# One core, attention, routed MLP and bilinear block: raw weight blocks side by side, split weights stored once and later, two units' weights made during attention, y stores issued by ScalarE

## The chip, the cores and the metric

The kernel runs on one core of one Trainium2 chip. The metric is the device time of one execution in microseconds (us). Of the kernel before, three timed runs gave a median of 2388.02 us (2387.21 to 2389.52).

## The reference

Three stages follow one another. The first is an attention with a decaying state, over 4 batches, 8 heads, 768 steps and head size 48:

```python
f = 1.0 / (1.0 + np.exp(-f_logit))
for t in range(S):
    state = f[:, :, t, :, None] * state + np.einsum('bhd,bhe->bhde', k[:, :, t], v[:, :, t])
    y[:, :, t] = np.einsum('bhd,bhde->bhe', q[:, :, t], state)
```

Its output, 3072 tokens by 384, goes through a layer of 8 experts that all compute on all tokens. The weights of the sum come from `P`, eight rounds of normalising rows and columns (Sinkhorn) of `exp(x @ w_gate)`:

```python
for e in range(E):
    h = np.maximum(x @ w1[e], 0.0)          # 384 -> 1024
    out += P[:, e:e + 1] * (h @ w2[e])      # 1024 -> 384
```

The last stage is `((x @ w_a) * (x @ w_b)) @ w_out` with a width of 1536. Its three weights arrive as 64-bit floats and are turned into 32-bit ones on the chip.

## The kernel before, in words

**Arithmetic.** Every matrix product of weights and activations is made of three TensorE passes over operands split into a high and a low part (`h` and `l` in the tile names): high by high, high by low, low by high. ScalarE makes a high part (a copy), GpSimd or VectorE the low part (a difference).

**Two plans.** The program is written as a list of steps (`Plan.add`: priority, engine, estimated cost, what is read and written, the call, and `late`, the time after which a transfer counts as landed). `Plan.order` (L116) walks through them with the estimated costs and fixes the order in which each engine gets its instructions; each engine then runs its list strictly in order and waits on semaphores. There are two plans. The first (L364 to L856) holds attention in 24 steps of 128 tokens, the MLP of expert 0 for each pair of steps (`expert0`, L648, all of its blocks but the last) and the start of the normalising of `P` (`sinkhorn`, L696). The second (L863 to L1101) holds everything else. All transfers of the kernel before are issued by the SP queue; its estimated cost of an issue lies between 0.05 and 1.09 us, and `LATE` is 4.0 us.

**Units of the second plan.** Its work is cut into 81 jobs (L747). A job of kind `moe` takes three blocks of 128 hidden columns for 1024 tokens; there are 19 of them for each of three groups of tokens. A job of kind `out` does the same for `w_a` or `w_b`. The order is: 19 moe jobs, 19 moe jobs, 8 out jobs, 19 moe jobs, 16 out jobs. A job's *front* (`front`, L902) computes three hidden blocks by two halves of 512 tokens with 15 products (`CHAINS`, L43) instead of 18, from 15 sums of activation blocks (tiles `xsh`, `xsl`) and 15 sums of weight blocks (tiles `w1h`, `w1l`; two sets, used in turn). ScalarE copies a product out of its bank pG (`z<-pG`), or VectorE adds it to another. The *back* (`back`, L979) splits the hidden blocks (`gh`, `gl`), multiplies by the second weight (`w2h`, `w2l`, from a 192 KB load into `raw`) in banks pR, and VectorE adds the result to `acc`. The back of a job is planned beside the front of a later one.

**Weights of a job.** Only the first time a weight unit is used are its sums made. Nine raw blocks of 128x128 go to nine of the 15 slots of the tile `stage`, in three steps (`W_RAW`, L23; `w1_load`, L762). For `moe` a step loads three blocks, each in two transfers of 64 rows (`moe_rows`, L271), so that a unit has 18 transfers of 32 KB. GpSimd makes 13 sums of slots (`W_SUMS`, `w1_split`, L786). Then, in three groups of five slots (`W_GROUPS`), ScalarE makes `w1h`, GpSimd makes `w1l`, and SP stores each half to HBM (`wfmoe..h`, `wfmoe..l`): six stores of 320 KB for a unit, planned right behind the group's split. Later jobs with the same unit load these stored parts, in six loads.

**Around the border of the two plans.** In attention the first unit's weights are made and 9 of the 15 activation sums (`NXA`, L201). The other six and unit 1's weights follow at the head of the second plan. Four of the eight normalising rounds are in the first plan (`ROUNDS1`). Expert 0's result is stored to HBM as `y0` by SP (L683), and loaded into `acc` by the second plan. The tiles of the second plan lie where those of attention lay, and wait for their last readers.

Of the kernel before, what the change touches and what calls it, by code (L numbers as in the profile page):

```python
# [22 lines left out]
W_RAW = [[14, 13, 8], [5, 1, 9], [6, 12, 3]]  # L23
W_SUMS = [
    (0, 1, "subtract", 9),
    (2, 3, "subtract", 0),
    (0, 0, "add", 8),
    (4, 9, "add", 3),
    (4, 4, "add", 5),
    (7, 5, "subtract", 8),  # L30
    (10, 14, "add", 6),
    (11, 10, "add", 13),
    (10, 10, "add", 8),
    (9, 2, "subtract", 11),
    (9, 9, "subtract", 12),
    (14, 14, "add", 13),
    (14, 5, "subtract", 14),
]
W_GROUPS = [(0, 5), (5, 10), (10, 15)]
# [44 lines left out]
class Plan:  # L84
# [11 lines left out]
    def __init__(self):  # L96
        self.ops = []
        self.last = {}
# [17 lines left out]
    def order(self, share):  # L116
# [15 lines left out]
        while any(todo.values()):  # L132
# [24 lines left out]
            for u in users[n]:  # L157
                gap = late + (self.GAP if self.ops[u][1] != eng else 0.0 if eng == "PE" else self.SAME)
# [8 lines left out]
def kernel(  # L167
# [33 lines left out]
    NXA = 9  # L201
# [6 lines left out]
    ROUNDS1 = 4  # L208
# [19 lines left out]
    w1s = [[big.tile([128, NW, 128], F32R, name=f"w1{x}0") for x in "hl"]]  # L228
# [47 lines left out]
    def add_piece(plan, prio, key, parts, hj, lj, reads=()):  # L276
# [10 lines left out]
        plan.add(prio, "SP", .05 + m * .0013, reads, [rk], get, LATE)  # L287
# [110 lines left out]
    def attention(s):  # L398
# [230 lines left out]
        op(ACT, .37, [f"xf{z}"], [xk], lambda: nc.scalar.activation(out=hi, in_=xf, func=AF.Copy))  # L629
# [18 lines left out]
    def expert0(b):  # L648
# [22 lines left out]
        for tt in range(EB // 128):  # L671
# [11 lines left out]
            op(SP, .55, [ky], [], lambda ys=ys, tt=tt: nc.sync.dma_start(  # L683
# [78 lines left out]
    def w1_load(plan, prio, n):  # L762
# [4 lines left out]
        if first_of[kind, u] != n:  # L767
            for g, (lo, hi) in enumerate(W_GROUPS):
                for x, t in enumerate((wh, wl)):
                    plan.add(prio + W_STEP * g, SP, .1, [f"wf{kind}{u}{x}{g}"], [f"w1{n % 2}{g}"], partial(  # L770
                        nc.sync.dma_start, out=f32(t[:, lo:hi]), in_=wfd[kind][u][x][:, lo:hi]), LATE)
            return
        for kk, slots in enumerate(W_RAW):
            def get(kk=kk, slots=slots):
                for slot, (e, c) in zip(slots, blocks):
                    if kind == "moe":
                        parts = moe_rows(e, c, 128)[kk]
                    else:
                        parts = [(0, 128, wd[e][kk * 128:kk * 128 + 128, c:c + 128])]
                    for p0, k, src in parts:  # L780
                        nc.sync.dma_start(out=stage[p0:p0 + k, slot, :], in_=src)  # L781

            reads = [f"wd{ab}"] if kind == "out" else []
            plan.add(prio, SP, .38, reads, [f"sg{x}" for x in slots], get, LATE)

    def w1_split(plan, prio, n):  # L786
# [10 lines left out]
        for g, (lo, hi) in enumerate(W_GROUPS):  # L797
# [7 lines left out]
            for x, t in enumerate((wh, wl)):  # L805
# [336 lines left out]
```

## Time and profile before

| what | value |
|---|---|
| median of 3 runs | 2388.02 us |
| the profiled execution | 2391.95 us |
| its span, first to last instruction | 2390.2 us |
| TensorE busy | 2204.8 us, 92% |
| VectorE, ScalarE, GpSimd busy | 70%, 44%, 47% |
| mean granted TensorE clock | 0.962 |

In the page, PE is TensorE, DVE VectorE, ACT ScalarE, POOL GpSimd, SP the SyncE queue (SPq its issuing of transfers); L1101 is the line from which the second plan's steps are called, so that most of that plan's instructions carry it and are told apart by their tiles. TensorE's share is an average over stages. The table by stage, with busy times, clock and transfers, shows where it is lower, and the waits say what ended its idle time there. Idle time of another engine costs nothing by itself.

### The profile page before, as it was taken

To read this page: it belongs to the slowest core of one execution; us is meant where nothing else is said; L and a number is where in the kernel's file an instruction comes from. 1 tells how busy PE (TensorE), PEld (TensorE's weight loads), DVE (VectorE), ACT (ScalarE), POOL (GpSimd) and SP (SyncE) were. 2 spreads that over 40 slices of the span, in tenths; PEclk is the share of its full clock that TensorE was granted. 3 is DMA by queue.
4 is the path that set the end of the run, shared out by engine and by line. 5 is a ranking of instruction groups with operands and counts; after the bars stand their busy time and mean duration, and the time that the engine had idled before them with its cause. 6 is when DMAs were issued, how large, how long until landed. Compare 5 with 4: busy or idle time off the path is not lost.

```text
span 2390.2 us, 41604 instructions
## 1 busy us (share of the span) xinstructions
PE 2204.8 (92%) x15100; PEld 1968.6 (82%) x15100; DVE 1673.1 (70%) x2939; ACT 1050.0 (44%) x2059; POOL 1114.3 (47%) x1127
## 2 busy tenths in 40 slices
PE   4999889978899889999889999999999999999998
PEld 3888788857777778898779998888899999988887
DVE  6888889655676766768998877668655555656755
ACT  3544555543333433453334446445444444533432
POOL 4112341156774655536553337774533333645522
PEclk5899999988999999999999999999999999999999
DMA  6445654244554434556665444547643333556641
GB/s 147 101 89 128 152 125 89 56 131 147 175 184 134 138 130 132 175 183 217 226 190 177 147 148 151 183 150 249 229 132 112 115 116 100 171 180 206 219 139 41
DMA packets 360206, 359.18 MB, mean 150 GB/s; under 512 B 154560, under 2 KB 261312, under 8 KB 360000
## 3 DMA queue, kind: packets, MB, share of 16 engines
q1 hardware_dynamic: 360000, 356.52, 49.0%
q8 instruction: 119, 1.95, 0.4%
q14 instruction: 87, 0.71, 0.1%
HBM read 252.19 MB, written 99.48 MB: 147 GB/s over the span
## 4 chain that ended last, share of the span: by engine, by line
PE 50%; DVE 7%; DMA 2%; POOL 2%; SPq 2%; issue 1%; ACT 0%; POOLq 0%; DVEq 0%; ACTq 0%
PE pR L310 26%; PE pG L924 18%; PE pF L924 6%; DVE z L1101 3%; SPq L781 1%; DVE gl L1101 1%; POOL stage L1101 1%; DMA z<-in_moe_w_b_dram 1%; POOL w1l L1101 1%; DVE z L257 1%; DVE acc L1101 0%; DVE z L259 0%; DMA stage<-in_moe_w_dram 0%; DVE xsl L1101 0%; DVE z L261 0%
## 5 line engine op out<-in xcount | busy, mean ns | idle before, releaser
L310 PE MATMUL pR<-w2h,gl 128*128 128x384 f32 x1656 | 567.3, 343 | 2.5 <-POOL gl L1101 2.0
L310 PE MATMUL pR<-w2l,gh 128*128 128x384 f32 x1656 | 566.5, 342 | 0.0
L310 PE MATMUL pR<-w2h,gh 128*128 128x384 f32 x1656 | 562.6, 340 | 3.4 <-ACT gh L1101 3.2
L1101 ACT ACTIVATE z<-pG 128x512 f32<-128x512 f32 x474 | 281.2, 594 | 460.9 <-PE pG L924 438.9
L924 PE MATMUL pG<-xsh,w1h 128*128 128x512 f32 x891 | 363.0, 407 | 100.7 <-ACT z L1101 60.0
L1101 POOL TENSOR_TENSOR gl<-z,gh 128x512 fp32r<-128x512 f32 x219 | 296.2, 1365 | 322.6 <-ACT gh L1101 232.2
L1101 DVE SCALAR_TENSOR_TENSOR acc<-pR,prob,acc 128x384 f32<-128x384 f32 x528 | 320.4, 611 | 147.2 <-PE pR L310 142.6
L924 PE MATMUL pG<-xsl,w1h 128*128 128x512 f32 x891 | 357.8, 402 | 0.9 <-DVE xsl L1101 0.9
L924 PE MATMUL pG<-xsh,w1l 128*128 128x512 f32 x891 | 356.6, 400 | 1.7 <-POOL w1l L1101 1.7
L310 PEld LDWEIGHTS pR<-w2h,gh 128*128 128x128 f32 x1656 | 316.3, 191 | 46.9 <-ACT gh L1101 3.8
L310 PEld LDWEIGHTS pR<-w2l,gh 128*128 128x128 f32 x1656 | 315.8, 191 | 40.2
L268 POOL TENSOR_TENSOR w2l<-raw,w2h 128x384 fp32r<-128x384 f32 x207 | 226.5, 1103 | 247.0 <-ACT w2h L266 237.6
L310 PEld LDWEIGHTS pR<-w2h,gl 128*128 128x128 f32 x1656 | 316.4, 191 | 4.1 <-POOL gl L1101 3.1
L1101 ACT ACTIVATE gh<-z 128x512 fp32r<-128x512 f32 x414 | 248.4, 624 | 144.5 <-DVE z L1101 85.2
L1101 DVE TENSOR_TENSOR z<-pF,z 128x512 f32<-128x512 f32 x324 | 222.1, 687 | 92.1 <-PE pF L924 61.7
L924 PEld LDWEIGHTS pG<-xsh,w1h 128*128 128x128 f32 x891 | 170.3, 191 | 134.2 <-ACT z L1101 70.9
L1101 DVE TENSOR_TENSOR z<-z,pG 128x512 f32<-128x512 f32 x243 | 166.2, 684 | 113.8 <-PE pG L924 110.0
L1101 POOL TENSOR_TENSOR stage<-stage 128x128 f32<-128x128 f32 x338 | 162.7, 511 | 168.8 <-DMA stage<-in_moe_w_dram 147.4
L1101 DVE SCALAR_TENSOR_TENSOR gl<-z,gh 128x512 fp32r<-128x512 f32 x171 | 165.3, 977 | 66.2 <-ACT gh L1101 66.2
L924 PEld LDWEIGHTS pG<-xsh,w1l 128*128 128x128 f32 x891 | 170.1, 191 | 41.0 <-POOL w1l L1101 2.2
L1101 DVE TENSOR_TENSOR z<-pG,z 128x512 f32<-128x512 f32 x174 | 119.8, 688 | 116.1 <-PE pG L924 113.2
L667 POOL TENSOR_TENSOR hl<-hf,hh 128x256 fp32r<-128x256 f32 x84 | 74.4, 887 | 248.8 <-ACT hf L665 215.8
(168 smaller groups left out, 3657.1 us busy)
## 6 DMA issues: line engine op xcount, KB each, us to landing
raw<-in_moe_w_dram SPq DMA_DIRECT2D x178, 192.0 KB, 2.8
l<-x2d SPq DMA_DIRECT2D x45, 256.0 KB, 3.4
stage<-in_moe_w_dram SPq DMA_DIRECT2D x342, 32.0 KB, 2.1
l<-x1d SPq DMA_DIRECT2D x32, 256.0 KB, 3.2
raw<-wd SPq DMA_DIRECT2D x36, 192.0 KB, 3.0
nat_f<-in_f_logit_dram SPq DMA_DIRECT2D x24, 192.0 KB, 3.5
nat_q<-in_q_dram SPq DMA_DIRECT2D x24, 192.0 KB, 3.7
nat_k<-in_k_dram SPq DMA_DIRECT2D x24, 192.0 KB, 4.0
```

What stands on the lines that cost most here:

```text
L257: lambda: stt(out=f32(t), in0=lo.bitcast(U32), scalar=2.0 ** -52, in1=f32(t), op0=ALU.mult, op1=ALU.mult),
L268: plan.add(prio + 1, "POOL", .1 + m * .0026, [gk, key], [key], lambda: nc.gpsimd.tensor_tensor(out=lj, in0=got, in1=f32(hj), op=ALU.subtract))
L310: nc.tensor.matmul(out=ps, lhsT=a[:, off:off + 128], rhs=b, start=(start and i == 0), stop=(stop and i == n - 1))
L667: op(POOL, .64, [f"hh{ft}", kf], [f"hl{ft}"], lambda hh=hh, hl=hl, hf=hf: nc.gpsimd.tensor_tensor(out=hl, in0=hf, in1=f32(hh), op=ALU.subt ...
L781: nc.sync.dma_start(out=stage[p0:p0 + k, slot, :], in_=src)
L924: nc.tensor.matmul(out=ps, lhsT=a[:, x], rhs=b, start=(new and i == 0), stop=(i == 2), skip_group_check=not new)
L1101: fn()
```

## The change

- A unit's raw blocks lie side by side in `stage`: slots 12 to 14, 3 to 5 and 6 to 8. Blocks of one expert that follow one another make one run, and a run is loaded in one transfer (two for `moe`, of 64 rows by 384 columns, 96 KB). A unit inside one expert has 6 transfers instead of 18; four of the units 2 to 18 (5, 8, 13 and 16) cross a border of experts and have 12. `W_SUMS` is renamed to the new slots, `W_OF` says in which slot a product's weight lies, and the groups have 6, 4 and 5 slots.
- The split weights are stored in two transfers of 983 KB (all 15 slots), planned at two thirds of the job that uses them, after its product 9, instead of six right after the split. The next split into the same set of tiles waits for these stores.
- The first two units' weights are made in attention, after steps 14 and 17, and not stored there. In exchange 5 instead of 9 activation sums are taken in attention and 10 at the head of the second plan, through tiles `z`, seven of them with VectorE.
- Two normalising rounds are in attention and six in the second plan.
- Expert 0's result is stored by ScalarE's queue.
- The plan's estimated costs of SP issues are changed, and its gap between engines in the second plan is 0.4 instead of 0.2.

```diff
-W_RAW = [[14, 13, 8], [5, 1, 9], [6, 12, 3]]
+W_OF = [0, 4, 1, 8, 2, 3, 6, 9, 14, 5, 10, 11, 7, 13, 12]
+W_RAW = [12, 3, 6]
...
-W_GROUPS = [(0, 5), (5, 10), (10, 15)]
+W_GROUPS = [(0, 6), (6, 10), (10, 15)]
...
-    NXA = 9
+    NXA = 5
...
-    ROUNDS1 = 4
+    ROUNDS1 = 2
...
-        plan.add(prio, "SP", .05 + m * .0013, reads, [rk], get, LATE)
+        plan.add(prio, "SP", .42 if m == DM else .85, reads, [rk], get, LATE)
...
-            op(SP, .55, [ky], [], lambda ys=ys, tt=tt: nc.sync.dma_start(
+            op(ACT, .35, [ky], [], lambda ys=ys, tt=tt: nc.scalar.dma_start(
                 out=y0[b * (EB // 128) + tt], in_=ys), 3.0)
...
-        for kk, slots in enumerate(W_RAW):
-            def get(kk=kk, slots=slots):
-                for slot, (e, c) in zip(slots, blocks):
+        runs = []
+        for f, (e, c) in enumerate(blocks):
+            if runs and runs[-1][1] == e and runs[-1][2] + runs[-1][3] == c:
+                runs[-1][3] += 128
+            else:
+                runs.append([f, e, c, 128])
+        for kk, slot in enumerate(W_RAW):
+            def get(kk=kk, slot=slot):
+                for f, e, c, m in runs:
...
-                        nc.sync.dma_start(out=stage[p0:p0 + k, slot, :], in_=src)
-
-            reads = [f"wd{ab}"] if kind == "out" else []
-            plan.add(prio, SP, .38, reads, [f"sg{x}" for x in slots], get, LATE)
+                        nc.sync.dma_start(out=stage[p0:p0 + k, slot + f:slot + f + m // 128, :].rearrange(
+                            "p s f -> p (s f)"), in_=src)
+
+            cost, reads = (1.2, []) if kind == "moe" else (.4, [f"wd{ab}"])
+            plan.add(prio, SP, cost * len(runs), [*reads, *after], [f"sg{slot + f}" for f in range(3)], get, LATE)
...
-            for x, t in enumerate((wh, wl)):
-                plan.add(at + 2, SP, .1, [f"w1{n % 2}{g}"], [f"wf{kind}{u}{x}{g}"], partial(
-                    nc.sync.dma_start, out=wfd[kind][u][x][:, lo:hi], in_=f32(t[:, lo:hi])), LATE)
+
+    def w1_store(plan, prio, n, after):
+
+        ph, u, _, _ = jobs[n]
+        kind = phases[ph][0]
+        if first_of[kind, u] == n:
+            for x, t in enumerate(w1s[n % 2]):
+                plan.add(prio, SP, .4, [after] + [f"w1{n % 2}{g}" for g in range(3)], [f"wf{kind}{u}{x}"], partial(
+                    nc.sync.dma_start, out=wfd[kind][u][x], in_=f32(t)), LATE)
...
-    w1_load(plan, 1000 * 12, 0)
-    w1_split(plan, 1000 * 12 + 600, 0)
+    for n in range(2):
+        w1_load(plan, 1000 * (15 + 3 * n), n, [f"st{14 + 3 * n}"])
+        w1_split(plan, 1000 * (15 + 3 * n) + 600, n)
...
-    plan = Plan()
+    plan = Plan(.4)
...
+        w1_store(plan, 1000 * n + SPREAD * 2 // 3, n, f"at{n}-9")
...
-        x_take(plan, -3000 + i, 0, i, POOL, l_of[i % 3])
-    w1_load(plan, -2500, 1)
-    w1_split(plan, -2000, 1)
+        z = idle[i][1:]
+        idle[i] = (1500, *z)
+        x_take(plan, -3000 + i, 0, i, POOL if i % 3 == 0 else DVE, z)
```

**The SP queue early in attention.** Before, after the third load of `nat_f`, unit 0's 18 block loads stand ahead of the loads of expert 0's second weight (`raw`):

```order
L411 DMA nat_f1_120<-in_f_logit_dram 128x8x48
L781 DMA stage_93<-in_moe_w1_dram 64x1x128 x12
L418 DMA Y0_127<-in_v_dram 64x4x48
L781 DMA stage_93<-in_moe_w1_dram 64x1x128 x6
L285 DMA raw1_95<-in_moe_w2_dram 128x384
L418 DMA Y1_128<-in_v_dram 64x4x48
L411 DMA nat_q1_122<-in_q_dram 128x8x48
```

In the changed kernel at the same place (its lines are two further down):

```order
L413 DMA nat_f1_114<-in_f_logit_dram 128x8x48
L420 DMA Y0_121<-in_v_dram 64x4x48
L287 DMA raw1_89<-in_moe_w2_dram 128x384
L420 DMA Y1_122<-in_v_dram 64x4x48
L413 DMA nat_q1_116<-in_q_dram 128x8x48
```

The block loads of `stage` are gone from here; 12 transfers for unit 0 and 6 for unit 1 stand later in attention.

**The SP queue at the border of the two plans.** Before, the last stores of `y0` stand ahead of the second plan's first loads, and 18 block loads of unit 1 behind three activation loads:

```order
L625 DMA x1d_99<-xf1_142 128x3x128
L683 DMA y0_98<-ys1_186 128x384
L683 DMA y0_98<-ys0_185 128x384
L683 DMA y0_98<-ys1_186 128x384
L1101 DMA l0_6531<-x1d_99 128x512
L1101 DMA l1_6532<-x1d_99 128x512
L1101 DMA l2_6533<-xf0d_101 128x512
L781 DMA stage_93<-in_moe_w1_dram 64x1x128 x18
```

In the changed kernel the ten activation loads, into tiles `z5` to `z14`, follow attention's last transfer at once (four of them are shown), and eight loads of `acc` and unit 2's blocks follow them:

```order
L627 DMA x1d_93<-xf1_136 128x3x128
L1119 DMA z5_6475<-xf0d_95 128x512
L1119 DMA z6_6476<-xf0d_95 128x512
L1119 DMA z7_6477<-xf0d_95 128x512
L1119 DMA z8_6478<-xf0d_95 128x512
...
L1119 DMA acc7_6524<-y0_92 128x384
L789 DMA stage_87<-in_moe_w1_dram 64x1x384 x6
```

The stores of `y0` are no longer in this queue, and unit 1's blocks have been loaded earlier.

**The SP queue over one unit of the first 19 jobs.** Before, with the stores of unit 3 around unit 4's block loads:

```order
L1101 DMA wfmoe3h_211<-w1h1_6485 128x640
L1101 DMA wfmoe3l_212<-w1l1_6486 128x640
L781 DMA stage_93<-in_moe_w1_dram 64x1x128 x18
L1101 DMA wfmoe3h_211<-w1h1_6485 128x640
L1101 DMA wfmoe3l_212<-w1l1_6486 128x640
L895 DMA wd0_107<-z19_6530 128x256
L285 DMA raw0_94<-in_moe_w2_dram 128x384
```

In the changed kernel, from the stores of unit 6 to those of unit 7:

```order
L1119 DMA wfmoe6h_211<-w1h0_83 128x1920
L1119 DMA wfmoe6l_212<-w1l0_84 128x1920
L910 DMA wd0_101<-z6_6476 128x256
L287 DMA raw1_89<-in_moe_w2_dram 128x384
L789 DMA stage_87<-in_moe_w1_dram 64x1x384 x4
L907 DMA z16_6486<-in_moe2_w_a_dram 128x512
L1119 DMA wfmoe7h_213<-w1h1_85 128x1920
L1119 DMA wfmoe7l_214<-w1l1_86 128x1920
L287 DMA raw0_88<-in_moe_w2_dram 128x384
```

The block loads are fewer, and two stores of 15 slots each (1920 columns) stand directly ahead of a load of `raw`. Their place follows product 9 of the same unit on TensorE. Between the last matmul of a job's product 9 and the first matmul of the job that uses the same set of weight tiles next, TensorE's list of the changed kernel has 33 matmuls of 512 columns and 57 of 384 (jobs 10 and 12). In the kernel before, from the last use of the first group of weight slots to its next use, it has 63 and 108.

## Rows read from the trace of the kernel before

**Rows 1.** Busy by stage: us, PE, PEld, DVE, ACT, POOL, clock, DMA share, GB/s

```profile
0.00:495.70 495.70, 425.28 (x6408) 383.23 (x6408) 392.85 (x862) 251.10 (x619) 139.31 (x159) 0.91 0.48 108
495.70:612.00 116.30, 86.62 (x361) 71.41 (x359) 70.69 (x122) 45.40 (x82) 75.77 (x91) 0.87 0.48 156
612.00:1019.00 407.00, 364.02 (x1735) 324.48 (x1736) 279.07 (x449) 156.34 (x279) 243.23 (x298) 0.95 0.46 153
1019.00:1487.00 468.00, 447.88 (x2247) 404.26 (x2246) 381.72 (x702) 205.85 (x373) 226.09 (x188) 0.99 0.56 180
1487.00:2390.20 903.20, 881.03 (x4356) 785.17 (x4354) 548.81 (x807) 391.35 (x707) 429.91 (x393) 0.99 0.48 156
```

**Rows 2.** Chain that ended last, second group of moe jobs: start, us, what

```profile
1357.71 1.58 PE pR L310 x9
...
1380.76 1.58 PE pR L310 x9
...
1405.44 1.39 PE pG L924 x6
```

**Rows 3.** Waits of ScalarE, 495 to 1019: total us, times, longest us

```profile
ACT w1h L1101 <- POOL stage L1101: 88.3, 27, 8.0
ACT w2h L266 <- DMA raw<-in_moe_w_dram: 61.5, 12, 11.1
```

**Rows 4.** Timeline of SP, 552 to 578: start, us, what, how many

```profile
552.34 12.25 SPq L781 DMA_DIRECT2D stage<-in_moe_w_dram  x18
...
577.87 0.55 SPq L781 DMA_DIRECT2D stage<-in_moe_w_dram  x1
```

**Rows 5.** Timelines of ScalarE and TensorE in that stretch: idle before in brackets

```profile
568.81 0.52 ACT L266 ACTIVATE w2h<-raw 128x384 fp32r<-128x384 f32 x1 [7.34 <-DMA raw<-in_moe_w_dram]
569.24 0.58 ACT L1101 ACTIVATE z<-pG 128x512 f32<-128x512 f32 x1
569.87 0.79 PE L924 MATMUL pG<-xsh,w1h 128*128 128x512 f32 x1 [4.87 <-ACT z L1101]
```

**Rows 6.** Chain that ended last, 880 to 1019: shares by line

```profile
by line: SPq L781 19.8%; PE pR L310 15.9%; POOL stage L1101 10.9%; PE pG L924 9.8%; POOL w1l L1101 9.2%; DMA stage<-in_moe_w_dram 7.5%; issue 6.6%; DVE gl L1101 2.9%; PE pF L924 2.5%; POOL w2l L268 2.1%; DVE z L1101 1.9%; DMA wd<-z 1.9%; DM
```

**Rows 7.** Timelines of SP, ScalarE, TensorE at attention's start

```profile
5.88 1.22 SPq L285 DMA_DIRECT2D raw<-in_moe_w_dram  x2
...
22.97 8.05 SPq L781 DMA_DIRECT2D stage<-in_moe_w_dram  x12
...
38.18 0.52 ACT L266 ACTIVATE wo0h<-raw 128x384 fp32r<-128x384 f32 x1 [10.02 <-DMA raw<-in_moe_w_dram]
...
39.24 1.10 PE L426 MATMUL pT<-ident,nat_k 128*112 128x128 f32 x4 [6.34 <-ACT e L431]
```

**Rows 8.** Timelines of SP and TensorE at the border of the plans

```profile
476.23 17.08 SPq L683 DMA_DIRECT2D y<-ys  x3
...
494.81 12.12 SPq L781 DMA_DIRECT2D stage<-in_moe_w_dram  x18
...
518.55 0.80 PE L924 MATMUL pG<-xsh,w1h 128*128 128x512 f32 x1 [9.23 <-ACT z L1101]
```

**Rows 9.** Waits of the SP queue, whole run

```profile
SPq L683 <- ACT ys L681: 32.2, 10, 12.8
```

**Rows 10.** A transfer by name: count, KB each, us from issue to landing

```profile
raw<-in_moe_w_dram SPq DMA_DIRECT2D x178, 192.0 KB, 2.8
```

**Rows 11.** Busy in three short stretches, columns as in rows 1

```profile
1140.00:1200.00 60.00, 50.62 (x252) 44.93 (x251) 55.00 (x92) 21.66 (x40) 36.27 (x27) 0.99 0.66 224
1320.00:1380.00 60.00, 60.00 (x307) 54.81 (x306) 49.47 (x105) 25.79 (x48) 24.49 (x19) 1.00 0.49 152
1160.00:1165.00 5.00, 5.00 (x28) 4.56 (x27) 2.71 (x9) 1.72 (x3) 1.69 (x2) 1.00 1.04 398
```

**Rows 12.** GpSimd and ScalarE by group: count, busy us, mean ns, idle before

```profile
L1101 POOL TENSOR_TENSOR w1l<-stage,w1h 128x640 fp32r<-128x640 f32 x42 | 68.2, 1637 | 5.7 <-ACT w1h L1101 5.7
L1101 ACT ACTIVATE w1h<-stage 128x640 fp32r<-128x640 f32 x42 | 30.9, 736 | 87.6 <-POOL stage L1101 78.2 <-PE pG L924 9.5
```

More of the change, by code (lines that the diff above doesn't have):

```diff
@@ L227 @@
     xsum = [[big.tile([128, TB], F32R, name=f"xs{x}{n}") for x in "hl"] for n in range(NXA)]
-    w1s = [[big.tile([128, NW, 128], F32R, name=f"w1{x}0") for x in "hl"]]
+    w1s = [[big.tile([128, NW, 128], F32R, name=f"w1{x}{n}") for x in "hl"] for n in range(2)]
     stage = big.tile([128, NW, 128], F32, name="stage")
@@ L628, in attention @@
         xk = f"x{s % 4}"
-        op(ACT, .37, [f"xf{z}"], [xk], lambda: nc.scalar.activation(out=hi, in_=xf, func=AF.Copy))
+        op(ACT, .37, [f"xf{z}"], [xk, f"st{s}"], lambda: nc.scalar.activation(out=hi, in_=xf, func=AF.Copy))
         op(DVE, .47, [f"xf{z}"], [xk], lambda: nc.vector.tensor_tensor(
@@ L760, with w1_load @@
         first_of.setdefault((phases[ph][0], u), n)
-    def w1_load(plan, prio, n):
+    def w1_load(plan, prio, n, after=()):
         ph, u, blocks, ab = jobs[n]
@@ L821, in x_make @@
                 (key, t), (kx, src) = tiles[step[0]], x_raw(ph, step[1])
-                plan.add(prio, SP, .7, [kx], [key], partial(nc.sync.dma_start, out=t, in_=src), LATE)
+                plan.add(prio, SP, .4, [kx], [key], partial(nc.sync.dma_start, out=t, in_=src), LATE)
                 continue
@@ L834, in x_make @@
             if i is not None:
-                plan.add(prio, SP, .7, [ko], [f"xf{ph}{i}"], partial(
+                plan.add(prio, SP, .4, [ko], [f"xf{ph}{i}"], partial(
                     nc.sync.dma_start, out=xfd[ph][i], in_=to), 3.0)
@@ L891, in convert @@
         src = (w_a, w_b, w_out)[n].bitcast(I32)[r0:r0 + 128, 2 * c:2 * c + 2 * m]
-        plan.add(prio, SP, .7, [after], [rk], lambda: nc.sync.dma_start(out=raw, in_=src), LATE)
+        plan.add(prio, SP, .4, [after], [rk], lambda: nc.sync.dma_start(out=raw, in_=src), LATE)
         for i, fn in enumerate(to_f32(raw, m, cva, cvt)):
             plan.add(prio + 1 + i, DVE, (.07 + m / 960) * (1 if i % 2 or i == 4 else .65), [rk], [ck], fn)
-        plan.add(prio + 9, SP, .2, [ck], [f"wd{n}"], lambda: nc.sync.dma_start(
+        plan.add(prio + 9, SP, .36, [ck], [f"wd{n}"], lambda: nc.sync.dma_start(
             out=wd[n][r0:r0 + 128, c:c + m], in_=f32(cva[:, :m])), 3.0)
@@ L919, in front, with mm @@
             kp, ps = banks[bank]
-            def mm(ps=ps, new=new, x=x):
+            slot = W_OF[x]
+            def mm(ps=ps, new=new, slot=slot, x=x):
                 xh, xl = xsum[x]
                 for i, (a, b) in enumerate(((wh, xh), (wh, xl), (wl, xh))):
-                    nc.tensor.matmul(out=ps, lhsT=a[:, x], rhs=b, start=(new and i == 0),
+                    nc.tensor.matmul(out=ps, lhsT=a[:, slot], rhs=b, start=(new and i == 0),
                                      stop=(i == 2), skip_group_check=not new)
-            g = [lo <= x < hi for lo, hi in W_GROUPS].index(True)
+            g = [lo <= slot < hi for lo, hi in W_GROUPS].index(True)
             plan.add(prio, PE, .232 * 3, [f"xs{x}", f"w1{n % 2}{g}"],
-                     [kp] + [f"job{n}"] * (x + 1 == len(CHAINS)), mm)
+                     [kp, f"at{n}-{x}"] + [f"job{n}"] * (x + 1 == len(CHAINS)), mm)
             late = 1000 * n + SPREAD * (x + 1) // len(CHAINS) + 100
@@ L1064 @@
                 for j in range(TPG):
-                    plan.add(1000 * n + 10 * j, SP, .55, [], [f"acc{j}"], partial(
+                    plan.add(1000 * n + 10 * j, SP, .36, [], [f"acc{j}"], partial(
                         nc.sync.dma_start, out=acc[j], in_=y0[g * TPG + j]), LATE)
```

46 lines of the change are left out of this document (23 added, 23 removed).

## The prediction

> **What bounds the kernel now.** I read the table by stage first [rows 1]. TensorE is busy 881.0 of 903.2 us after 1487 us, at clock 0.99: little can be won there. The second group of moe jobs (1019 to 1487) stands idle for 20 us. The first group, cut after its first four units at 612, is the weak place: 116.3 and 407.0 us long, with 29.7 and 43.0 us of idle TensorE and mean clocks of 0.87 and 0.95. Attention, the first 495.7 us, has 70.4 us of idle TensorE.
>
> What a unit costs when nothing is late is seen in the chain of the second group [rows 2]: the same piece returns after 1380.76 - 1357.71 = 23.05 us. This agrees with its matmuls: 45 of 512 columns at 1.39/6 = 0.232 us and 72 of 384 at 1.58/9 = 0.176 us make 23.1 us. Fifteen units at 23.05 us are 345.8 us, so the stretch from 612 to 1019 loses 61 us: 43 idle and 18 by the lower clock that follows the idle time. The first four units, of which two have no back beside them (72 x 0.176 = 12.6 us each), should take 4 x 23.05 - 2 x 12.6 = 67 us and take 116.3: 49 lost, 29.7 idle and 19.6 by the clock. An idle us there costs 61/43 = 1.4 us in all, and 49/29.7 = 1.7 at the head.
>
> Then I followed one unit. SP needs 12.25 us to issue 18 block loads, 0.68 us each, and the next unit's begin 25.5 us after the last one's [rows 4]. The load of a second weight waits behind them in the same queue; ScalarE stands 7.34 us for it; the copy of a bank comes behind that conversion, and TensorE stands 4.87 us for the copy [rows 5]. So "PE waits for ACT" is really "SP is late". The waits of ScalarE over all 19 units agree: 88.3 us for GpSimd's sums, themselves behind the blocks, and 61.5 us for second weights [rows 3]. The chain at the end of the group says it outright: the block loads' issuing is its largest part, 19.8%, before TensorE's own 15.9% [rows 6].
>
> **The change part by part.**
>
> *Six loads for 18.* The cost to SP goes with the number of rows, not with their width: early in attention two loads of 64 rows by 512 columns take it 1.22 us, 0.61 each, against 8.05/12 = 0.67 for 64 by 128 [rows 7]. Six loads of 64 by 384 then take 6 x 0.68 = 4.1 us instead of 12.25, and two stores stand for six. SP's loop of 25.5 us loses over 8 us and falls below 23.05: it no longer sets the pace. GpSimd is busy 243.2/15 = 16.2 us per unit and VectorE 279.1/15 = 18.6 [rows 1], so TensorE becomes the bound. The four units with 12 loads need 8.2 us and fit as well.
>
> *What is late next: the stores.* They now hold the weight tiles. From the end of product 9 to the next use of the set stand 33 matmuls of 512 columns and 57 of 384: 33 x 0.232 + 57 x 0.176 = 17.7 us, where 63 and 108 gave twice as much. In that time SP issues both stores (0.7 us), they move 1.97 MB and land, ScalarE makes the high parts of six slots (0.74 x 6/5 = 0.9 us) and GpSimd the low parts (1.64 x 6/5 = 2.0 us) [rows 12]. No row shows so large a transfer. Between 1140 and 1200 the queues moved 224 GB/s at a share of 0.66, so 339 GB/s when full, and 398 in the best 5 us [rows 11]: 4.9 to 5.8 us of moving, and about 2 us to land, a little less than the 2.8 us of a whole 192 KB load [rows 10]. The sum is 0.7 + 5.8 + 2 + 0.9 + 2.0 = 11.4 us of 17.7. The tiles are ready in time.
>
> But the load of `raw` directly behind the stores lands some 5.8 + 2.8 = 8.6 us after the first store's issue, while the plan counts 4.0 us and the issues, about 5.5. ScalarE, placed by that plan, will stand about 3 us there once per unit. In the row above a stand of 7.34 us cost TensorE 4.87, so some 2.5 us are absorbed; the bounds are 0 and 3 us of idle TensorE per unit. I take 1.0, nearer the row, times 1.4 for the clock: 15 x 1.4 = 21 us remain of 61. **Saved: 40 us**, bounds 61 (all hidden) and -2 (3 us each).
>
> The Trainium skill ("DMA: Bandwidth & Descriptors", section "Anatomy of one DMA") gives a fit for the gpsimd path of 2.0 us plus bytes over 436 GB/s. By it both stores would have moved in 4.5 us, the stand would be some 1.3 us shorter and the sum about 10 us larger; no run here has moved 436 GB/s.
>
> *The head of the second plan.* The 18 loads of unit 1 (12.12 us) and the wait that held SP 17.08 us in three `y` stores both leave the way; TensorE's 9.23 us stand behind them goes [rows 8], and the 4.87 us stand of unit 2 [rows 5]. In exchange ten activation copies by ScalarE come in a row where six came before, four more at 0.6 us = 2.4 us, and seven differences by VectorE. Two more normalising rounds lie in the second plan; `acc` needs their result only when the first back is done, and they hide beside the fronts; unhidden, they cost some 10 us. Idle time falls by 14.1 - 2.4 = 11.7, times 1.7 = **20 us saved**, bounds 5 and 30.
>
> Why the queue of the `y` stores matters: SP, in order, stood 32.2 us for the tiles that ScalarE fills [rows 9]. The Trainium skill (the same page, section "Issuing engines are not separate DMA queues") says that issuing from another engine saves only the sequencer's issue time. By that rule the move alone would be worth 24 issues, and with only unit 1's loads gone the head would save about 12 us instead of 20.
>
> *Attention.* At its start the 18 loads of unit 0 hold SP, ScalarE stands 10.02 us behind them and TensorE 6.34 [rows 7]. They now come late in attention, in as many transfers for two units, where GpSimd has room (139.3 us busy of 495.7) [rows 1]; if that cover failed, unit 1's 13 sums and three splits, about 11 us, would show. ScalarE issues 24 stores; no row has an issue from ScalarE. The bounds are 0, hidden beside its 50% load, and 24 x 0.68 = 16 us at the dearest issue above. I take 2, since ScalarE's idle time covers most. **Saved: 7 us**, bounds -10 and 14.
>
> *The rest.* The planner's new costs reorder the later stages; what TensorE computes there is the same, and there it loses little. The second group's 30 us over 19 x 23.05 = 438 come from VectorE's conversion of the 64-bit weights and stay. I cost this 0, bounds +-8 us; the eight out jobs of the first out stage, with their shorter turns, could lose some of it to the stores.
>
> **Sum.** 40 + 20 + 7 = 67 us off the profiled execution's 2391.95: 2325. The median of the runs stands 3.9 us lower: **2321 us**.
>
> **Rivals.** (a) *All of it hides*: copies lag without TensorE noticing. Then 61 + 28 + 10 = 99 us go: 2289. For it speaks that the second group runs at 60.00 of 60 us with VectorE at 49.5 [rows 11]; against it, the stores ahead of the `raw` loads. 17%.
>
> (b) *The late stores take the place of the block loads*: each unit loses 3 us idle, times 1.4, as much as now; 20 + 7 - 2 = 25 us go: 2363. For it: the plan's count of 4.0 us. Against: ScalarE has waited twice a unit so far, and would wait once. Half of this loss gives 2340 to 2345. 18% for more than that half. The Trainium skill (the same page, "Queues, rings and completion order") says that descriptors of a ring are taken in order on each DMA engine, which would put the small load behind the whole of both stores; the rows show no such pair.
>
> (c) *SP was not the bound*: VectorE or GpSimd paces the unit. Between 1140 and 1200, with VectorE at 55.0 of 60, TensorE lost 9.4 us in 60 [rows 11]. At such a rate the 15 units would take 346 x 60/50.6 = 410 us and nothing would be won there: 2361. Against: 18.6 us of VectorE in 23.05 is 81%, and at 49.5/60 = 82% TensorE was busy throughout. 5%.
>
> (d) *Slower*: the weight tiles come free too late. It decides from 17.7 us on: if stores plus splits take longer, every first use waits. To eat all the savings, 15 units and eight out jobs would have to lose over (40 + 20 + 7 + 21)/23 = 3.8 us each in all, 2.7 idle, so that the turn takes 20.4 us and the stores 9.0 us longer than my sum: 1.97 MB in 14.8 us, 133 GB/s. With one more us of idle time on each, 23 x 1.4 = 32 us, the time is 2388 + 32 = 2420. The mean rate of that stretch is 153 GB/s [rows 1], everything included, and the pair has the queue nearly to itself. 5%.
>
> (e) *The change doesn't do what it says* can be left out: its order shows six loads and two stores.
>
> **How the numbers follow.** The forecast has 55%, and (a) 17%, (b) 18%, (c) 5%, (d) 5%. The predicted time is the forecast's. Its own range, with half of each bound, is 2298 to 2345. The range reaches half way into (a) and up to (c), 2286 to 2361, and leaves some 2 in 10 outside. About 0.2%, 5 us, is what a measurement here can tell from no change. Faster by more: 93%, all but (d) and the last of (b) and (c). Within: 2%. Slower: 5%.
>
> **What would show it.** Six block loads in about 4 us; the stretch of units 4 to 18 at 24 to 25 us per unit, with a clock near 1.0; the first front matmul near 488; ScalarE's waits for GpSimd's sums gone, and those for `raw` or the split tiles about 3 us once a unit. The prediction is wrong if a 96 KB load costs SP several times 0.68 us, if TensorE's idle time in the first group stays above 60 us, or if a new wait, for a split or a store, ends it.

## The result, and the profile after

| | median, us | runs | ratio, 95% interval |
|---|---|---|---|
| before | 2387.61 | 4 (2385.60 to 2389.52) | |
| changed | 2323.14 | 4 (2317.62 to 2328.94) | 0.973 [0.9702, 0.9759] |
| changed, again, beside the experiments | 2317.04 | 4 (2313.40 to 2321.78) | 0.9702 [0.9681, 0.9722] |

The change saves about 64 us, 2.7%. The profiled execution of the changed kernel took 2317.62 us, its span 2315.7. The table by stage of the changed kernel, cut at the same events as [rows 1] (the first product of job 0, of job 4, of job 19, of job 38); columns as there:

```profile
0.00:495.80 495.80, 433.06 (x6404) 391.29 (x6405) 391.81 (x854) 249.93 (x617) 145.22 (x171) 0.90 0.47 106
495.80:598.00 102.20, 84.33 (x371) 69.05 (x370) 76.31 (x138) 47.00 (x85) 76.01 (x89) 0.93 0.60 206
598.00:941.20 343.20, 342.08 (x1729) 310.92 (x1729) 289.98 (x448) 157.27 (x278) 242.93 (x282) 1.00 0.50 173
941.20:1407.20 466.00, 449.21 (x2250) 406.77 (x2249) 381.91 (x702) 207.51 (x373) 227.82 (x190) 0.99 0.57 179
1407.20:2315.70 908.50, 879.59 (x4354) 783.30 (x4352) 542.17 (x807) 392.06 (x706) 433.25 (x391) 0.99 0.48 157
```

Read the lengths against [rows 1]: attention is as long as before (495.8 for 495.7), units 0 to 3 take 102.2 us for 116.3, units 4 to 18 take 343.2 for 407.0, the second group 466.0 for 468.0. The remaining stages take 908.5 for 903.2. TensorE is busy 342.08 of the 343.2 us of units 4 to 18 at clock 1.00: 22.9 us a unit, so no idle time is left to win there. The head gained 14 of the 49 us that the prediction counted as lost in it, and attention is no shorter.

The waits of ScalarE from 495 to 941, which answer to [rows 3]:

```profile
ACT w1h L1119 <- POOL stage L1119: 14.0, 7, 2.6
ACT w2h L268 <- DMA raw<-in_moe_w_dram: 8.9, 3, 4.4
```

They were 88.3 and 61.5 us: of both waits that SP's block loads caused little is left, and the 8.9 us for `raw` lie in the head. The transfers by name (count, KB each, us from issue to landing) show why, and also what the larger transfers cost:

```profile
stage<-in_moe_w_dram SPq DMA_DIRECT2D x84, 96.0 KB, 2.4
wfmoe6h<-w1h SPq DMA_DIRECT2D x1, 960.0 KB, 4.5
wfmoe6l<-w1l SPq DMA_DIRECT2D x1, 960.0 KB, 6.3
y<-ys ACTq DMA_DIRECT2D x24, 192.0 KB, 2.2
```

And SP's timeline over one unit, the answer to [rows 4] (start, us, what, how many):

```profile
662.25 0.42 SPq L1119 DMA_DIRECT2D wfmoe6h<-w1h  x1
662.72 0.42 SPq L1119 DMA_DIRECT2D wfmoe6l<-w1l  x1
668.31 0.32 SPq L910 DMA_DIRECT2D wd<-z  x1
668.74 0.37 SPq L287 DMA_DIRECT2D raw<-in_moe_w_dram  x1
674.26 2.46 SPq L789 DMA_DIRECT2D stage<-in_moe_w_dram  x4
676.77 0.58 SPq L907 DMA_DIRECT2D z<-in_moe_w_a_dram  x1
677.39 0.43 SPq L1119 DMA_DIRECT2D wfmoe7h<-w1h  x1
677.87 0.43 SPq L1119 DMA_DIRECT2D wfmoe7l<-w1l  x1
678.40 2.38 SPq L287 DMA_DIRECT2D raw<-in_moe_w_dram  x2
680.87 2.20 SPq L789 DMA_DIRECT2D stage<-in_moe_w_dram  x2
```

Four loads of 96 KB take 2.46 us, 0.61 each, where twelve of 32 KB took 8.05 [rows 7]. SP now stands idle between its pieces (663.14 to 668.31, 669.11 to 674.26): it waits for the others, where they waited for it. The stores landed 4.5 and 6.3 us after their issue, so this pair was there 6.8 us after the first issue; for units 4 to 16 it was 6.3 to 7.8.

The last two lines show a price that nobody had put in: right behind a pair of stores, two loads of `raw` held SP for 2.38 us and two of `stage` for 2.20, 1.1 to 1.2 each, where they cost 0.37 and 0.61 a few lines above. It is so where loads follow the pair at once (in units 0 to 5 and 7); why was not tried.

### The profile page after: what moved, and what is told of

It is laid out like the page before. It is cut to its first block, busy times and chain, and to the rows that moved or that the text cites. A ratio compares the mean times of both kernels' runs of the same rounds, so it can differ in the third digit from the quotient of the medians.

```text
span 2315.7 us, 41003 instructions
## 1 busy us (share of the span) xinstructions
PE 2188.3 (94%) x15100; PEld 1961.3 (85%) x15100; DVE 1682.2 (73%) x2946; ACT 1053.8 (46%) x2059; POOL 1125.2 (49%) x1120
## 4 chain that ended last, share of the span: by engine, by line
PE 73%; DVE 17%; DMA 4%; issue 2%; ACT 2%; SPq 1%; POOL 0%; POOLq 0%; ACTq 0%; DVEq 0%
PE pR L312 35%; PE pG L940 23%; PE pF L940 8%; DVE z L1119 3%; PE pM L300 2%; PE pM L312 2%; DVE fi L451 1%; DVE X L508 1%; DVE gl L1119 1%; DMA z<-in_moe_w_b_dram 1%; DVE X L557 1%; SPq L622 1%; DMA xf<-q 1%; PE pA L471 1%; DVE acc L1119 1%
## 5 line engine op out<-in xcount | busy, mean ns | idle before, releaser
L940 PE MATMUL pG<-xsh,w1h 128*128 128x512 f32 x891 | 357.1, 401 | 42.0 <-DVE z L1119 34.7
L270 POOL TENSOR_TENSOR w2l<-raw,w2h 128x384 fp32r<-128x384 f32 x207 | 233.2, 1133 | 266.9 <-ACT w2h L268 232.8
L1119 DVE TENSOR_TENSOR z<-pG,z 128x512 f32<-128x512 f32 x174 | 119.8, 688 | 112.3 <-PE pG L940 109.9
L1119 DVE SCALAR_TENSOR_TENSOR gl<-z,gh 128x512 fp32r<-128x512 f32 x171 | 172.3, 1019 | 21.3 <-ACT gh L1119 19.8
L1119 POOL TENSOR_TENSOR stage<-stage 128x128 f32<-128x128 f32 x325 | 171.1, 554 | 17.4 <-DMA stage<-in_moe_w_dram 13.0
```

What stands on the lines that cost most here:

```text
L270: plan.add(prio + 1, "POOL", .1 + m * .0026, [gk, key], [key], lambda: nc.gpsimd.tensor_tensor(out=lj, in0=got, in1=f32(hj), op=ALU.subtract))
L940: nc.tensor.matmul(out=ps, lhsT=a[:, slot], rhs=b, start=(new and i == 0), stop=(i == 2), skip_group_check=not new)
L1119: fn()
```

## The experiments

All times below are medians, compared with runs of the kernel before on the same chip (median 2387 to 2392 us there). The stages come from one profile of each kernel; I call the first four units the head.

| kernel | ratio to before, 95% | attention | head | units 4 to 18 |
|---|---|---|---|---|
| before | 1 | 495.7 | 116.4 | 406.8 |
| e6: planner's costs alone | 0.995 [0.9932, 0.9969] | 488.3 | 113.4 | 403.6 |
| e9: late stores alone | 1.001 [0.9993, 1.0026] | 493.5 | 119.8 | 405.1 |
| e12: new layout, 18 loads | 0.9941 [0.9921, 0.9961] | 491.2 | 119.2 | 380.5 |
| e1: new layout, 6 loads | 0.9693 [0.965, 0.9737] | 492.3 | 93.1 | 349.1 |
| e2: changed, but 18 loads | 0.9873 [0.9829, 0.9918] | 501.6 | 118.1 | 361.1 |
| changed, first and second profile | 0.973 and 0.9702 | 495.8, 490.4 | 102.2, 104.9 | 343.3, 343.1 |
| e3: changed, early stores | 0.9681 [0.9648, 0.9713] | 492.6 | 99.4 | 341.6 |
| e4: changed, y stores on SP | 0.9708 [0.9673, 0.9742] | 489.7 | 106.7 | 343.4 |
| e5: changed, unit 1 at the head | 0.9695 [0.9674, 0.9717] | 492.7 | 101.1 | 347.1 |
| mix, twice | 0.965 and 0.9627 | 500.2, 488.2 | 94.7, 92.7 | 346.6, 346.3 |

**The loads alone.** The kernel before, with the blocks side by side and loaded by runs:

```diff
-W_RAW = [[14, 13, 8], [5, 1, 9], [6, 12, 3]]
+W_RAW = [12, 3, 6]
...
-W_GROUPS = [(0, 5), (5, 10), (10, 15)]
+W_GROUPS = [(0, 6), (6, 10), (10, 15)]
...
-                        nc.sync.dma_start(out=stage[p0:p0 + k, slot, :], in_=src)
+                        nc.sync.dma_start(out=stage[p0:p0 + k, slot + f:slot + f + m // 128, :].rearrange(
+                            "p s f -> p (s f)"), in_=src)
```

> The kernel before with one part of the change alone: raw blocks side by side, so six loads of 64 by 384 a unit (12 where it crosses a border of experts) instead of 18; stores, attention and the planner's costs as before (the three groups have 6, 4 and 5 slots). Theory A (SP's issuing set the pace of units 4 to 18): SP's 12.25 us a unit become 4 to 5, the waits of ScalarE for second weights (61.5 us) and for GpSimd's sums (88.3 us) fall below 40 together, the stretch of units 4 to 18 goes from 407 us to 345 to 365, attention gains up to 6 at its start, and the time is 2315 to 2345. Theory B (the loads matter little, and what helped was the later stores or the new order that the planner's costs make): the stretch stays above 390 us and the time above 2370.

Measured: 2319.36 us, as fast as the whole change. Theory A held. Its table by stage, head and units 4 to 18, columns as in [rows 1]:

```profile
492.30:585.40 93.10, 81.11 (x361) 67.71 (x361) 74.00 (x122) 46.26 (x83) 79.02 (x98) 0.95 0.65 211
585.40:934.50 349.10, 344.97 (x1736) 313.49 (x1736) 295.37 (x449) 157.16 (x278) 251.09 (x292) 1.00 0.52 172
```

Idle time of TensorE over the 15 units fell from 43.0 to 4.1 us, and the clock is 1.00. The head, 93.1 us, is even shorter than in the whole change.

**The changed kernel with 18 issues.** Same order on every engine; each load is cut in three:

```diff
-                for f, e, c, m in runs:
+                for f, e, c, m in [(f + i, e, c + 128 * i, 128) for f, e, c, m in runs for i in range(m // 128)]:
```

> The changed kernel with every engine's order of work unchanged, but each load of 384 columns issued as three of 128: 18 issues a unit again. Theory A (SP's issuing set the pace): units 4 to 18 go back from 343 us to 390 to 410, the late loads of raw and the waits for GpSimd's sums return (over 100 us for ScalarE together), and the time is 2365 to 2400. Theory B (order and stores made the gain): the stretch stays below 360 us and the time within 15 us of the changed kernel's 2323.

Measured: 2362.51 us, 361.1 us for units 4 to 18. It lies between the two theories: by the ratios the 12 more issues a unit cost 34 to 41 us in all. Only 18 us of that lie in units 4 to 18, where the kernel before is 58 us longer than e1; 13 to 16 lie in the head. Something else in the changed kernel bears 18 loads better. The next three runs looked for it.

**Late stores alone.** The kernel before, its six stores replaced by two behind product 9:

```diff
-            for x, t in enumerate((wh, wl)):
-                plan.add(at + 2, SP, .1, [f"w1{n % 2}{g}"], [f"wf{kind}{u}{x}{g}"], partial(
-                    nc.sync.dma_start, out=wfd[kind][u][x][:, lo:hi], in_=f32(t[:, lo:hi])), LATE)
...
+        w1_store(plan, 1000 * n + SPREAD * 2 // 3, n, f"at{n}-9")
```

> The kernel before with the other half of the pair alone: 18 loads a unit as before, but two whole stores behind product 9 of the unit that uses the weights, in place of six right behind the split; costs, attention and head as before. It fills the table of loads (18, 6) by stores (early, late), in which units 4 to 18 take 407 us (18, early), 349 (6, early), 361 (18, late, in the changed kernel's order) and 343 (6, late). Theory A (SP's time is what both halves give: six early stores make SP stand in line for the split, 64 us for the low parts and 11 us for the high parts over the 15 units, and late stores take this off as six loads take off 8 us a unit): the stretch takes 355 to 375 us, the waits of SP's stores for the split are gone, and the time is 2335 to 2365. Theory B (the 361 come from something else in the changed kernel, such as the y stores or unit 1 in attention): the stretch stays above 390, the time at 2375 or more.

Measured: 2392.29 us, and 405.1 us for the stretch. Theory A fell, B's numbers came, and the waits of SP over the 15 units tell how. Before:

```profile
SPq L1101 <- POOL w1l L1101: 63.8, 29, 4.6
...
SPq L781 <- POOL w1l L1101: 17.9, 8, 3.5
```

With late stores:

```profile
SPq L781 <- POOL w1l L1109: 86.4, 23, 9.5
```

SP stands for the same event, the end of GpSimd's low part. Where it stood in the stores it now stands in the block loads, which wait for their slots to be read out. Taking away the wait of one instruction only hands it to the next one in the queue.

**The planner's costs alone.** The kernel before with the new numbers and 4.0 us for a step of six block loads (one of the changed costs is shown):

```diff
...
-            plan.add(prio, SP, .38, reads, [f"sg{x}" for x in slots], get, LATE)
+            plan.add(prio, SP, 4.0 if kind == "moe" else 1.2, reads, [f"sg{x}" for x in slots], get, LATE)
...
```

> The kernel before with nothing changed but the planner's numbers: the new costs of SP issues, the gap of 0.4 in the second plan, and 4.0 instead of 0.38 for a step of six block loads. 18 loads a unit, six early stores, y on SP, one unit made in attention. Theory A (with the true cost in the plan SP puts loads of raw ahead of the blocks, and this is why the 18 loads cost only 18 us in the order of the changed kernel): units 4 to 18 go from 407 to 355 to 380, the time to 2340 to 2372. Theory B (the order does nothing; the fewer stores and the y stores off SP did it): the stretch stays above 390, the time at 2375 or more.

Measured: 2377.03 us, 403.6 us for the stretch. A fell. B's numbers came, but not its account: the order does something, and late stores alone (above) and `y` on SP (below) are worth nothing that can be told. The waits of ScalarE in that stretch did fall, from 78.2 and 40.2 us to

```profile
ACT w1h L1102 <- POOL stage L1102: 34.7, 18, 2.7
ACT w2h L267 <- DMA raw<-in_moe_w_dram: 12.2, 5, 5.5
```

so a plan with these costs does put the loads in a better order. TensorE still stands idle for 36.0 us, now in many short waits:

```profile
PE pG L925 <- DVE z L1102: 28.9, 36, 1.5
PE pG L925 <- ACT z L1102: 6.8, 10, 0.8
```

The new order has products stand for VectorE's sums. What in the plan brings that about was not tried.

**Layout without fewer issues.** The kernel of e1 with the cut of e2, so that e1's two parts are told apart:

> The kernel of e1_six_loads (the kernel before with blocks side by side and groups of 6, 4 and 5 slots), in the same order on every engine, but each load of 384 columns issued as three of 128. It parts the count of issues from the new layout of slots and groups, which e1 changed together, and from which the 361 us of e2 could come, since neither the costs (404 us) nor the late stores (405 us) alone gave them. Theory A (the count of issues is what e1 gained): units 4 to 18 take 385 to 410 us again, the head 110 to 118, the time is 2370 to 2392. Theory B (the layout gave most of it: the new order in which slots are freed and filled): the stretch takes 350 to 370 us, the time 2325 to 2350, and the six loads themselves are worth only the 10 to 20 us that are left.

Measured: 2375.31 us; head 119.2 and units 4 to 18 380.5 us. A held for the time and for what gained most; the stretch lies between the two theories. Of e1's gain of 73 us, 12 to 14 belong to the new slots and groups and about 59 to the issues, by the ratios 0.9941 and 0.9693. In the profiles the layout takes 26 us off units 4 to 18 and gives some back elsewhere; six issues take 31 more there and 26 in the head. Both kernels move the same bytes; the DMA engines are busy 0.48 and 0.52 of the stretch, and a load lands 2.1 us (32 KB) or 2.5 us (96 KB) after its issue; this speaks against the smaller transfers' own time as what the 18 lose.

```profile
491.20:610.40 119.20, 85.56 (x361) 70.78 (x359) 73.74 (x122) 46.00 (x83) 78.23 (x97) 0.89 0.50 164
610.40:990.90 380.50, 357.31 (x1734) 319.39 (x1735) 279.76 (x449) 157.03 (x278) 243.85 (x293) 0.97 0.48 158
```

Why the layout helps can be read in the code: a step of block loads used to fill slots of two or three groups, and waits for the low parts of all of them; now each step fills slots of one group. That this is the cause was not tried by itself. If the layout is worth the same in both orders, it accounts for 26 of the 46 us by which the changed kernel with 18 issues (361.1) was better than the kernel before. The other 20 stay open: late stores and new costs gave 2 and 3 us alone, and the other parts were not tried with 18 loads.

**Early stores in the changed kernel.** The two whole stores planned right behind the split:

```diff
-        w1_store(plan, 1000 * n + SPREAD * 2 // 3, n, f"at{n}-9")
...
+            w1_store(plan, 1000 * n + W_STEP // 2 + 122 + 2 * W_STEP, n + 2)
```

> The changed kernel with the two 983 KB stores planned right behind the split instead of behind product 9 of the unit that uses it (the first two units' stores then lie in attention). Theory A (SP's issuing alone mattered, stores are hidden wherever they lie): within 8 us of the changed kernel's 2323, units 4 to 18 at 343 to 350 us. Theory B (the later place is worth something, since stores ahead of a load of raw or of stage hold it back): units 4 to 18 lose 1 to 3 us each, 358 to 388 us, and the time is 2338 to 2370.

Measured: 2313.37 us, units 4 to 18 341.6 us. Theory B fell. A's account held, with numbers just below its ranges: with six loads SP has time to stand, and the place of the stores is worth nothing that can be told.

**Stores issued three times.** The changed kernel, with more bytes in the stores' turn:

```diff
...
+                    for _ in range(3):
+                        nc.sync.dma_start(out=wfd[kind][u][x], in_=f32(t))
...
```

> The changed kernel with each of the two late stores issued three times, so 5.9 MB instead of 1.97 MB a unit (the plan's order is the same). It measures the slack that the sum of the stores' turn gave: 11.4 us of 17.7. Theory A (that sum is right): two more pairs add 9 to 12 us, the turn takes 20 to 23 us and is 3 to 6 us too long, and units 4 to 18 take 343 + 15 x 1.4 x (3 to 6) = 405 to 470 us; the time is 2380 to 2460, with TensorE or ScalarE waiting on the stores. Theory B (the turn has much more room than 17.7 us, since only ScalarE's split waits for it and the set is wanted later): the stretch stays below 360 and the time below 2345. Theory C (the raw loads behind the stores decide first): ScalarE's waits for raw grow beyond 60 us while the split tiles are still in time.

Measured: 2629.23 us; units 4 to 18 501.2 us. That is 10.5 us a unit more, beyond the 4 to 8 that A gives with its factor for the clock. By the waits it is C first (ScalarE stood 120.4 us for raw), but the split tiles were not in time either: single waits of the split on the stores took 9 to 17 us. But the run does not measure the slack: SP's timeline shows that each repeated store waited for the one before it,

```profile
708.27 8.47 SPq L823 DMA_DIRECT2D wfmoe5h<-w1h  x3
716.79 10.45 SPq L823 DMA_DIRECT2D wfmoe5l<-w1l  x3
727.34 0.38 SPq L287 DMA_DIRECT2D raw<-in_moe_w_dram  x1
```

and its waits over units 4 to 18 name it for this unit:

```profile
SPq L823 <- DMA wfmoe5l<-w1l: 9.2, 2, 5.2
```

so SP itself was held for 19 us. It shows once more that a held SP costs this kernel its time; the 6 us of room that the sum gave to the stores stay unmeasured.

**The parts at the border.** The stores of y back on SP:

```diff
-            op(ACT, .35, [ky], [], lambda ys=ys, tt=tt: nc.scalar.dma_start(
+            op(SP, .55, [ky], [], lambda ys=ys, tt=tt: nc.sync.dma_start(
```

> The changed kernel with the stores of y issued by SP again, with SP's cost in the plan as before. Theory A (the head of the second plan gained by the free SP queue): the first front matmul or the first four units come 5 to 12 us later, 2328 to 2335. Theory B (the move cost ScalarE in attention as much as it gave the head): attention ends 5 to 10 us earlier, the head is as much longer, 2320 to 2326. Theory C (it only cost): attention ends 5 to 10 us earlier and the head stays, 2313 to 2319.

Measured: 2321.54 us (2311.00 to 2324.88): no difference that can be told. The time lies in B's range, but neither attention (489.7 us) nor the head (106.7) moved by B's 5 to 10.

Unit 1's weights at the head of the second plan:

```diff
-    for n in range(2):
+    for n in range(1):
         w1_load(plan, 1000 * (15 + 3 * n), n, [f"st{14 + 3 * n}"])
...
+    w1_load(plan, -2500, 1)
+    w1_split(plan, -2000, 1)
```

> The changed kernel with unit 1's weights made at the head of the second plan instead of in attention (the tiles stay where they are). Theory A (making it in attention hides): the head gets 4 to 12 us longer, attention stays, 2324 to 2335. Theory B (attention pays for it in its last third, where its early lead of 13 us is lost): attention ends 5 to 10 us earlier and the head gets as much longer, within 5 us of the changed kernel. Theory C: attention gains more than the head loses, 5 to 12 us below it.

Measured: 2318.05 us, beside 2317.04 for the changed kernel in the same group of runs. The time is B's, without B's shift: neither attention nor the head moved (492.7 and 101.1 us). With six loads a unit fits in either place. The changed kernel was run as the anchor of that group:

> The changed kernel itself once more, beside the others of this group, so that they can be compared on one chip: 2315 to 2330 by either theory.

**A version that beats both.** Six loads, two early stores as in e3, y on ScalarE and the new costs, but attention and head as in the kernel before:

```diff
-    NXA = 5
+    NXA = 9
...
-    ROUNDS1 = 2
+    ROUNDS1 = 4
...
+    w1_load(plan, 1000 * 12, 0)
+    w1_split(plan, 1000 * 12 + 600, 0)
+    w1_store(plan, 1000 * 12 + 622 + 2 * W_STEP, 0)
```

> Parts put together anew: six loads, two whole stores right behind the split, y stores from ScalarE and the planner's new costs, but attention and head as in the kernel before (unit 0 early in attention, unit 1 at the head, 9 sums and 4 normalising rounds in attention). Theory A (the head of the run with six loads alone, 93 us, comes from its 9 sums and 4 rounds in attention, and the planner's new order gives 342 for units 4 to 18): the stretches add up to about 492 + 93 + 342 + 465 + 157 + 750 = 2299, so 2296 to 2310. Theory B (the head differs by chance of the order, and all versions with six loads are the same): 2311 to 2325.

> The kernel of the run e8_mix once more, for a second profile and a second comparison with the kernel before: if its 2304 us was no accident of one group of runs, 2296 to 2310 again, with attention at 490 to 495 where the first profile showed 500, the head at 93 to 95 and units 4 to 18 at 342 to 347.

Measured: 2303.64 us (2295.90 to 2326.12, 6 runs), ratio 0.965 [0.9616, 0.9684]; again 2301.67 us (2294.43 to 2308.39, 5 runs), 0.9627 [0.9603, 0.9651]. The interval of the first group of runs just meets that of the changed kernel ([0.9681, 0.9722]); the second lies clear below it. By the ratios 12 to 18 us are gained, and the second profile shows 10 to 12 of them in the head, 92.7 us for 102.2 and 104.9:

```profile
0.00:488.20 488.20, 429.58 (x6408) 387.01 (x6408) 386.62 (x862) 252.24 (x619) 135.06 (x159) 0.97 0.49 112
488.20:580.90 92.70, 81.06 (x361) 66.54 (x360) 76.40 (x120) 45.11 (x82) 82.07 (x98) 0.95 0.59 198
580.90:927.20 346.30, 344.36 (x1736) 313.49 (x1735) 291.95 (x451) 158.15 (x279) 251.04 (x292) 1.00 0.51 175
```

All kernels with 5 sums and 2 rounds in attention and six loads have a head of 99 to 107 us (but for the one with tripled stores), all with 9 and 4 one of 93 to 95. It is not unit 1's place (e5 has the head of the changed kernel). Whether it is the sums, the rounds, unit 0's place or the engine that makes the low parts of the sums was not parted.

## Why the prediction was right, and where not

The total was right (2321 us forecast, 2323 and 2317 measured; 2325 and 2317.6 for the profiled execution), and so was its cause: SP's issuing of block loads. Three of its four terms were off, in ways that partly cancel, so that the sum came this near is in part luck. By the profiles: 63.5 + 14.2 - 0.1 - 3.2 = 74.4 us, for 40 + 20 + 7 + 0 = 67. The upper end of the stated range, 2345, does not follow from its working: half of each bound on the slow side adds up to 41 us, 2362.

- **Six loads for 18: 40 forecast, 64 measured** in units 4 to 18. The price of an issue was right: 0.61 us for 64 by 384, as for 64 by 128. That it goes with the number of rows was not: a `raw` load of 128 by 384 costs 0.37 us (668.74 above), less than one of 64 rows; the block loads' source has a shape of its own (64x1x384), and which of the two makes the price was not tried. All issues of SP in units 4 to 18 add up to 226 us before and 112 after, 7.6 us a unit less. TensorE became the bound at 22.9 us a unit. The step that failed is "ScalarE, placed by that plan, will stand about 3 us there once per unit", which left 21 of the 61 us lost. The raw loads behind the stores did land late; from the first store's issue (677.39) to the first landing it is some 8.4 us, as reckoned (8.6). The view of `raw` from 674 to 696 gives the two issues, and their time to landing (shortest, median, longest):

```profile
L287 SPq DMA_DIRECT2D raw<-in_moe_w_dram x2: 1093/1142/1192, 678.4 to 679.6; - x2
DMA to landing us min/median/max: 6.9/7.1/7.4
```

  But ScalarE took up these two loads only here:

```profile
705.93 0.53 ACT L268 ACTIVATE w2h<-raw 128x384 fp32r<-128x384 f32 x1 [0.61 <-PE pR L312]
707.64 0.52 ACT L268 ACTIVATE w2h<-raw 128x384 fp32r<-128x384 f32 x1
```

  That is 20 us after they had landed. I priced a late landing without asking how long before its use the load is issued. In units 4, 5 and 15, too, raw loads followed the stores within 3 us and landed 4.4 to 6.2 us after their issues. In nine units (6, 8 to 14 and 16) SP stood for VectorE's conversion between the stores and the load (663.14 to 668.31 above), so that the load met no store at all. ScalarE's wait for raw in units 4 to 18 is nothing, not 45 us. Rival (a), everything hides, was right for this stretch.
- **The stores' turn.** I reckoned 8.5 us from the first issue to the landing of both; it was 6.3 to 7.8 in units 4 to 16. The split into the freed tiles did not wait for them, here at 671.46, 2.4 us after the landing, nor in any other of units 4 to 18:

```profile
671.46 0.84 ACT L1119 ACTIVATE w1h<-stage 128x768 fp32r<-128x768 f32 x1
```

  The Trainium skill ("DMA: Bandwidth & Descriptors", section "Anatomy of one DMA") gives 2.0 us plus bytes over 436 GB/s for the gpsimd path. By it I estimate 6.5 us for the pair as one transfer: nearer to the 6.8 above than my sum, though these stores were issued by SP.
- **The head: 20 forecast, 14 measured**, and for the wrong reasons. I gave the gain to the y stores' wait and to unit 1's loads leaving SP. The y stores moved back change nothing, nor does unit 1's move. Six issues for 18 make 26 us there (119.2 to 93.1), and what the changed kernel does otherwise at the border takes 5 to 12 back; the 2.4 us that I priced for that was too small. TensorE's idle time in the head fell by 11.8 us (29.7 to 17.9), as summed (11.7), though not for those reasons, so this is luck; its busy time fell by 2.3 us (86.62 to 84.33) and not by the 8 that the factor 1.7 adds for the clock (0.87 before, 0.93 after). The wait of the y stores was not removed either, it changed its form. SP waits at the border for the landing of ScalarE's last two stores:

```profile
SPq L1119 <- DMA y<-ys: 16.6, 2, 13.2
```

  The timeline shows which loads stand: not those of `acc`, which read `y0`, but the seventh and eighth of the ten activation loads. Their tiles `z` lie where attention's tiles lay, and wait for the last readers of those, here the stores (issued at 492.8 and 496.5, landed 1.9 us later):

```profile
479.58 1.89 SPq L1119 DMA_DIRECT2D z<-x1d  x2
494.71 4.98 SPq L1119 DMA_DIRECT2D z<-xf0d  x4
499.80 4.63 SPq L1119 DMA_DIRECT2D acc<-y  x8
```

  The Trainium skill (the same page, section "Issuing engines are not separate DMA queues") says that another issuing engine saves only the sequencer's time. The runs agree as far as they can tell: the move is worth nothing that shows (2321.5 us with the stores on SP).
- **Attention: 7 forecast, 0 and 5 measured** in two profiles. The early stand did go: by ScalarE's copies `q<-pO` the first eight steps come 7 to 24 us earlier. In the first profile the lead is gone by step 19, in the second some 5 us are left. TensorE's idle time in attention fell by 7.7 and 10.6 us, about as forecast (from 70.4 to 62.7 and 59.8), but its busy time rose by 7.8 and 5.4 us, from 425.28 to 433.06 and to that of the second profile:

```profile
0.00:490.40 490.40, 430.64 (x6404) 389.21 (x6405) 390.17 (x854) 250.13 (x617) 144.97 (x171) 0.96 0.47 107
```

  The clock alone does not explain that (0.91 before, 0.90 and 0.96 after); why the same matmuls are busy longer stays open. The two profiles of the mix (below) differ by 12 us in attention, so one profile cannot judge a term of 7. ScalarE's issues of y cost 0.33 to 0.40 us each, 24 of them 8.0 us, within the bounds; my 2 us for what shows can't be checked.
- **The rest: 0 forecast, 3 us longer.** The last 16 out jobs take 320 to 323 us in every kernel with the new layout and 315.6 to 316.8 in the three with the old one (before, e6, e9), from the first product of the first of them to the end; near the end a pair of jobs takes 34.3 us there, 33.3 to 33.8 with the old. That is a price of the layout that I didn't see.
- **Rivals.** (b), late stores in the place of the loads, did not come, though its order shows: the raw load at 678.40 landed at 685.8, just behind the stores at 685.2. It cost nothing, and early and late stores are alike. (c) fell: VectorE is busy 290 of the 343 us of units 4 to 18, and TensorE stands 1.1 us in all. (d) did not come; its point of decision stays unmeasured.

## What to carry to other kernels

Where one in-order queue issues everything, count its issues per turn of the loop: transfers of 64 rows cost the same time whether they are 128 or 384 columns wide, and merging them was worth about 59 us, more than all the other edits together. A wait taken off one instruction of such a queue goes to the next (late stores alone: nothing), as long as the loop itself stays as long. A late landing costs only what is left after the distance between issue and use, so read that distance before pricing it, and judge parts that are put in together by running each alone.

## What was not expected of the hardware

The same kernel, with the same idle time of TensorE, had attention of 488.2 and of 500.2 us. The first row is above; the other profile of the mix reads

```profile
0.00:500.20 500.20, 441.59 (x6408) 397.79 (x6408) 387.82 (x862) 252.52 (x619) 136.01 (x159) 0.92 0.48 109
```

Idle time is 58.6 us in both; the granted clock is 0.97 and 0.92, and TensorE is busy 12 us longer. In attention two single executions differ by this much without any difference in the program.
